# Chunk attention into a Swish layer: head order of the q and k loads, and the order of VectorE's work between TensorE's products

## The chip, the cores and the metric

The kernel runs on one core of a Trainium2 chip. The metric is the time of one execution in microseconds (us), as the device measures it; the span of a profile, from the first to the last instruction, is about 2 us shorter. TensorE multiplies matrices, VectorE (DVE in the profile), ScalarE (ACT) and GpSimd (POOL) work elementwise, and SyncE (SP) issues transfers. GpSimd issues transfers too. A run more than 1.5% above the fastest of its kernel is called slow and is left out of the ratios.

## The reference

```python
# q, k, v: [8 batches, 8 heads, 576, 64] float32, attention within chunks of 64 rows
scores = q_c @ k_c.T / 8
attn = softmax(scores)
x = (attn @ v_c)  -> [4608 tokens, 512]      # heads side by side
h = x @ w_in                                 # [512, 2048]
g = h / (1 + exp(-beta * h))                 # beta: [2048]
out = g @ w_out                              # [2048, 512], float32
```

## The kernel before

The tokens go through in nine blocks (`j`) of 512. A block has attention (scores, exp, a product with v, a division), 16 first-layer tiles (`emit_m`: four products of 128x512, then tanh on ScalarE and the gate on VectorE) and a second layer. Block 0 has a plain second layer; the others use a Strassen scheme: 7 groups of 16 products instead of 8, for which VectorE forms sums `s1` to `s4` of the gated tiles and GpSimd forms sums `tw` of the weights once. The loop puts the attention of block j+1 and the Strassen products of block j-1 into block j, at m = 4. A batch has 576 rows, a block 512.

```python
    def load_qk(b):
        ...
        for z in range(2):
            for src, dst in ((q, q_t), (k, k_t)):
                nc.gpsimd.dma_start(
                    out=dst[b][:, z].rearrange("p r d -> p (r d)"),
                    in_=src[b].rearrange("(a z) (t r) d -> z a t (r d)", z=2, r=RUN)[z],
                )
    ...
    def emit_sums(j, a, n):          # n = 4: four additions of 128x1024 in a row
        ...
        tt(out=s1[:, lo], in0=g[:, lo, dn], in1=g[:, hi, dn], op=ALU.add)
        tt(out=s2[:, lo], in0=s1[:, lo], in1=g[:, lo, up], op=ALU.subtract)
        tt(out=s3[:, lo], in0=g[:, lo, up], in1=g[:, lo, dn], op=ALU.subtract)
        tt(out=s4[:, lo], in0=g[:, hi, up], in1=s2[:, lo], op=ALU.subtract)
    ...
        def st6():                   # end of a block's Strassen products
            prod("A", s1, t1, False, True)
            o = ...                  # ScalarE: o = 0.5 * A
            put(1, 1, o)
            nc.gpsimd.tensor_tensor(out=w_, in0=sb["w1"], in1=o, op=ALU.add)
            put(0, 1, comb("C", w_)) # VectorE: waits for GpSimd
    ...
        for j in range(1, NB):
            at = attn(j + 1) if j + 1 < NB else []
            for m in range(KFF):
                if m == 4 and j >= 2:
                    for n, st in enumerate(steps_L2(j - 1)):
                        st()
                        if at and n < 6:
                            at.pop(0)()
                    if j + 2 < B:
                        for h2 in range(2):
                            emit_T(j + 2, h2)   # four q/k transposes on VectorE
                        ...                     # loads of batch j + 3
                if j == 1 and m >= 4 and at and m % 2 == 0:
                    at.pop(0)()
                emit_m(j, m)
                if m in (11, 15):
                    emit_sums(j, m - 11, 4)
```

The softmax here doesn't subtract the row's maximum and nothing guards it: scores larger than these inputs give would overflow.

## Time and profile before

| | before |
|---|---|
| time, median of the first 3 runs | 375.06 us |
| span of the profile | 373.1 us |
| TensorE / VectorE busy | 290.0 / 220.1 us |
| full-width first-layer products begin (block 0) | 29.3 us |
| first Strassen product | 110.4 us |
| from one block's first Strassen product to the next | 38.1 to 39.5 us in blocks 2 to 5, then 32.7 us, the last 24.6 us |

From the page of the kernel before: busy time of each engine with its share of the span, and the clock granted to TensorE in 40 slices, in tenths.

```profile
PE 290.0 (78%) x3296; PEld 173.5 (47%) x3296; DVE 220.1 (59%) x354; ACT 140.0 (38%) x216; POOL 83.8 (22%) x82
PEclk9999999569769989996999899989999999999999
```

No engine is full, and the clock falls again and again. What TensorE waited for, from the waits of the kernel before (engine and line, what released it: us in total, times, the longest):

```profile
PE hps L194 <- DVE gt L205: 23.8, 10, 3.9
PE sc L137 <- DVE kT L118: 19.0, 3, 14.3
PE oA L257 <- DVE gt L205: 10.4, 8, 1.4
```

The first-layer products (`hps`) and the first Strassen product (`oA`) wait for gates (`gt`), because a gate frees the PSUM bank that the next tile needs. The gates are late since VectorE does other things first. The timeline of the kernel before at one block's end shows them (start, us, engine, line, what, and in brackets the idle time before it and what ended it):

```profile
204.34 1.27 POOL L314 TENSOR_TENSOR w<-w,o 128x512 f32<-128x512 f32 x1 [3.19 <-issue]
205.64 0.69 DVE L275 SCALAR_TENSOR_TENSOR osb<-oC,w 128x512 f32<-128x512 f32 x1 [2.98 <-POOL w L314]
206.25 1.25 DVE L118 STREAM_TRANSPOSE qT<-qu 128x576 f32<-128x576 f32 x1
...
209.50 1.24 DVE L118 STREAM_TRANSPOSE kT<-ku 128x576 f32<-128x576 f32 x1
210.58 2.46 DVE L205 SCALAR_TENSOR_TENSOR gt<-sg,hps 128x512 f16<-128x512 f32 x4
211.31 8.75 PE L194 MATMUL hps<-xt,w_in 128*128 128x512 f16 x32 [3.90 <-DVE gt L205]
```

VectorE stands 2.98 us until GpSimd has its sum, combines, makes four transposes (4.3 us), and only then comes to the four gates that have been ready. TensorE is idle for 3.90 us. After that the clock is low, by the busy time in stretches (columns: stretch and its length, busy us of PE, PEld, DVE, ACT and POOL with instruction counts, granted clock, DMA share, GB/s):

```profile
211.30:214.70 3.40, 3.39 (x9) 1.27 (x9) 2.43 (x4) 1.38 (x2) 0.00 (x0) 0.53 0.97 158
```

The start, from the timeline of the kernel before: the first q is in VectorE's hands at 10.98 us.

```profile
10.98 1.26 DVE L118 STREAM_TRANSPOSE qT<-qu 128x576 f32<-128x576 f32 x1 [9.43 <-DMA qu<-in_q_dram]
29.33 16.26 PE L194 MATMUL hps<-xt,w_in 128*128 128x512 f16 x64 [0.52 <-DVE xt L181]
```

### The profile page before, as it was taken

What the parts mean: (1) busy time and instruction counts of PE and PEld (TensorE: products, weight loads), DVE (VectorE), ACT (ScalarE), POOL (GpSimd) and SP (SyncE); (2) the same over time, 40 slices, a digit from 0 to 9 for tenths busy, and PEclk for the clock granted to TensorE, in tenths of its full rate; (3) what the DMA queues carried; (4) which work ended last, traced back from release to release, by engine and by line L of the source; (5) the groups of instructions that cost most, each with busy time, mean ns of one, the idle gap of its engine ahead of it and who ended that gap; (6) DMA issues with size and microseconds to landing.
All of it is one profiled execution on the core that took longest, in us unless ns stands there. A gap on an engine that the chain in (4) does not pass through costs nothing.

```text
span 373.1 us, 7694 instructions
## 1 busy us (share of the span) xinstructions
PE 290.0 (78%) x3296; PEld 173.5 (47%) x3296; DVE 220.1 (59%) x354; ACT 140.0 (38%) x216; POOL 83.8 (22%) x82
## 2 busy tenths in 40 slices
PE   0149995479589867995889588958899699889893
PEld 0133442334138523862367136723674386367382
DVE  0544705387892579347852886378636934961951
ACT  1114701227323345332633263236427533633620
POOL 7324398513000520043002500110011002002002
PEclk9999999569769989996999899989999999999999
DMA  5999998699903599239912790320032023002002
GB/s 61 179 207 199 191 155 149 96 98 130 113 7 60 109 134 62 60 89 148 69 44 74 133 115 26 80 68 2 2 100 71 2 60 108 6 18 70 29 28 86
DMA packets 81827, 32.02 MB, mean 86 GB/s; under 512 B 65921, under 2 KB 76161, under 8 KB 81793
## 3 DMA queue, kind: packets, MB, share of 16 engines
q0 software_dynamic: 57216, 18.40, 48.7%
q1 hardware_dynamic: 24576, 13.12, 13.6%
q8 instruction: 26, 0.43, 0.5%
q14 instruction: 9, 0.07, 0.1%
HBM read 36.71 MB, written 9.44 MB: 124 GB/s over the span
## 4 chain that ended last, share of the span: by engine, by line
PE 48%; DVE 32%; issue 8%; ACT 4%; DMA 4%; POOL 3%; POOLq 0%; DVEq 0%
PE hps L194 17%; PE oA L257 13%; DVE gt L205 8%; PE oD L257 4%; PE oB L257 4%; DVE qT L118 4%; DMA vb<-in_v_dram 4%; DVE kT L118 3%; PE ops L323 3%; PE sc L137 3%; DVE s L219 3%; DVE x L167 3%; DVE s L220 3%; DVE s L222 2%; DVE s L221 2%
## 5 line engine op out<-in xcount | busy, mean ns | idle before, releaser
L194 PE MATMUL hps<-xt,w_in 128*128 128x512 f16 x576 | 144.6, 410 | 29.1 <-DVE gt L205 23.8
L202 ACT ACTIVATE sg<-hps,beta 128x512 f32<-128x512 f32 x144 | 99.0, 688 | 97.0 <-PE hps L194 55.9
L194 PEld LDWEIGHTS <-w_in 128*128 128x128 f16 x576 | 59.2, 104 | 108.8 <-issue 54.5
L205 DVE SCALAR_TENSOR_TENSOR gt<-sg,hps 128x512 f16<-128x512 f32 x144 | 93.0, 681 | 22.2 <-ACT sg L202 22.0
L302 POOL TENSOR_TENSOR w<-u,u 128x512 f32<-128x512 f32 x8 | 10.1, 1268 | 222.7 <-ACT u L268 222.7
L257 PEld LDWEIGHTS <-s 128*128 128x128 f16 x512 | 48.1, 98 | 6.3
L257 PE MATMUL oA<-tw,s 128*128 128x256 f16 x384 | 46.0, 273 | 0.0
L257 PEld LDWEIGHTS <-gt 128*128 128x128 f16 x384 | 36.5, 98 | 18.0 <-issue 12.6
L146 ACT ACTIVATE et<-sc 128x512 f16<-128x512 f32 x36 | 19.5, 594 | 44.9 <-PE sc L137 44.4
L137 PE MATMUL sc<-qT,kT 32*64 32x64 f16 x1152 | 14.6, 201 | 20.6 <-DVE kT L118 19.0
L268 ACT ACTIVATE u<-oA 128x512 f32<-128x512 f32 x24 | 14.3, 597 | 42.4 <-PE oA L257 42.4
L167 DVE TENSOR_TENSOR x<-x,rd 128x512 f16<-128x512 f32 x36 | 24.9, 691 | 1.2
L275 DVE SCALAR_TENSOR_TENSOR osb<-oD,u 128x512 f32<-128x512 f32 x8 | 5.5, 692 | 33.8 <-ACT u L268 33.8
L118 DVE STREAM_TRANSPOSE qT<-qu 128x576 f32<-128x576 f32 x16 | 19.9, 1241 | 9.4 <-DMA qu<-in_q_dram 9.4
L137 PEld LDWEIGHTS <-kT 32*64 32x64 f16 x1152 | 12.1, 114 | 25.1 <-DVE kT L118 19.3
L257 PE MATMUL oA<-w_out,gt 128*128 128x256 f16 x128 | 15.3, 272 | 10.4 <-DVE gt L205 10.4
L275 DVE SCALAR_TENSOR_TENSOR osb<-oC,w 128x512 f32<-128x512 f32 x8 | 5.5, 692 | 26.3 <-POOL w L314 26.3
L118 DVE STREAM_TRANSPOSE kT<-ku 128x576 f32<-128x576 f32 x16 | 19.8, 1236 | 0.8 <-DMA ku<-in_k_dram 0.8
L91 POOL DMA_DIRECT2D vb<-in_v_dram x16 | 18.7, 1173 | 5.6 <-DMA w_out<-in_moe_w_out_dram 5.4
L159 PE MATMUL x<-vb,et 64*64 64x65 f16 x576 | 13.3, 208 | 7.8 <-DVE x L167 3.3
L165 DVE RECIPROCAL rd<-x 128x8 f32<-128x8 f32 x36 | 7.3, 204 | 16.0 <-PE x L159 16.0
L159 PEld LDWEIGHTS <-et 64*64 64x64 f16 x576 | 8.6, 114 | 17.0 <-DVE x L167 6.7
(38 smaller groups left out, 192.4 us busy)
## 6 DMA issues: line engine op xcount, KB each, us to landing
out_dram<-osb SPq DMA_DIRECT2D x28, 256.0 KB, 2.2
qu<-in_q_dram POOLq DMA_DIRECT2D x16, 288.0 KB, 11.5
ku<-in_k_dram POOLq DMA_DIRECT2D x16, 288.0 KB, 11.7
vb<-in_v_dram POOLq DMA_DIRECT2D x16, 288.0 KB, 13.2
w_in<-in_moe_w_in_dram POOLq DMA_DIRECT2D x4, 512.0 KB, 15.7
w_out<-in_moe_w_out_dram POOLq DMA_DIRECT2D x4, 512.0 KB, 16.7
out_dram<-o SPq DMA_DIRECT2D x8, 256.0 KB, 4.1
xt<-x SPq DMA_TRANSPOSE x28, 2.3
```

The lines of the kernel that those rows point to most:

```text
L91: nc.gpsimd.dma_start(out=t[64 * hp:64 * hp + 64, :, :, 0:D].rearrange("p s c d -> p (s c) d"), in_=v[b, 4 * hp:4 * hp + 4].rearrange("s ( ...
L118: nc.vector.transpose(out=dst[b][:, h2].rearrange("p t r e -> p (t r e)").bitcast(FP32).rearrange("p (t r) -> p r t", r=RUN), in_=src[b][: ...
L137: nc.tensor.matmul(out=sc[a % 2][o0:o0 + 64, z, c, :], lhsT=kk[:, cb * CH:(cb + 1) * CH, e], rhs=qq[:, cb * CH:(cb + 1) * CH, e], start=(e ...
L146: nc.scalar.activation(out=et, in_=sc[s], func=ACTF.Exp, scale=scale)
L159: nc.tensor.matmul(out=x[o0:o0 + 64, hp, s, 0:D + 1], lhsT=et_t[g, a2][p0:p0 + 64, z, 2 * (i % 2) + cp, :], rhs=vbuf[b % NV][p0:p0 + 64, s ...
L167: nc.vector.tensor_tensor(out=x16, in0=x[:, :, :, 0:D], in1=rd.to_broadcast([128, 2, 4, D]), op=ALU.mult,)
L194: nc.tensor.matmul(out=hps, lhsT=w[:, kk, m // 2, m % 2, :], rhs=xt_t[j][:, kk, :], start=(kk == 0), stop=(kk == KDM - 1),)
L202: nc.scalar.activation(out=sg, in_=hps, func=ACTF.Tanh, scale=beta2[:, m % 2, m // 2:m // 2 + 1])
L205: nc.vector.scalar_tensor_tensor(out=gt_t[j][:, m, :], in0=sg, scalar=1.0, in1=hps, op0=ALU.add, op1=ALU.mult)
L219: tt(out=s1[:, lo], in0=g[:, lo, dn], in1=g[:, hi, dn], op=ALU.add)
L257: nc.tensor.matmul(out=bank[name][:, i, :], lhsT=a[:, kk, i * 128:(i + 1) * 128], rhs=b[:, kk, :], start=(first and i == 0 and kk == 0), s ...
L268: nc.scalar.activation(out=sb[name], in_=bank[src], func=ACTF.Copy, scale=0.5)
```

## The change

Four intents. Head order "(z a)" makes the source of a q or k load one 128-long dimension, which is meant to spread it over all 16 DMA engines. VectorE's sums are halved and given out one per gate; transposes and combinations stand each beside a group of Strassen products, and the C combination no longer waits for the last GpSimd sum. Batch 1's attention moves into block 0's plain second layer. All of w_in and w_out is loaded ahead of batch 1. The core of the diff (the head order also permutes w_in's rows and the indices of v; not shown either are the copies after TensorE's transposes, moved from VectorE to ScalarE, and two buffer counts):

```diff
-    def load_qk(b):
+    def load_qk(b, split=False):
...
-        for z in range(2):
+        for zs in ((slice(0, 1), slice(1, 2)) if split else (slice(0, 2),)):
             for src, dst in ((q, q_t), (k, k_t)):
                 nc.gpsimd.dma_start(
-                    out=dst[b][:, z].rearrange("p r d -> p (r d)"),
-                    in_=src[b].rearrange("(a z) (t r) d -> z a t (r d)", z=2, r=RUN)[z],
+                    out=dst[b][:, zs].rearrange("p z r d -> p z (r d)"),
+                    in_=src[b].rearrange("(z a) (t r) d -> (a t) z (r d)", z=2, r=RUN)[:, zs],
                 )
...
+        def cC():
+            comb("C", sb["w1"], keep="t")      # needs nothing of the last product
...
+            # mm6: out = t + o on GpSimd, on VectorE in the last block
...
+        emit_sc(0)
+        emit_sc(1, spare=True)                  # both score groups first, in spare PSUM
...
+        for m in range(2):
+            emit_h(0, m, 0, HT)                 # half-width products ahead of the last pv
+        emit_pv(3, True)
...
+        hooks = {                               # inside block 0's plain second layer
+            8: lambda: [T1[0](), T1[1]()], 9: lambda: [T1[2](), T1[3]()],
+            10: lambda: emit_sc(2), 12: lambda: emit_pv(4, True), 13: lambda: emit_pv(5, True),
+            14: lambda: emit_sc(3), 15: lambda: emit_pv(6, True),
+        }
...
+                    mm[0]()
+                    for p in range(4):
+                        emit_sum(j - 1, 3, p)
+                    if at:
+                        at[0]()
+                    if tr:
+                        tr.pop(0)()             # one transpose
+                    mm[1]()
+                    cB()
...
+                    mm[5]()
+                    if at:
+                        at[5]()
+                    cC()
+                    if tr:
+                        tr.pop(0)()
+                    mm[6]()
...
                 emit_m(j, m)
-                if m in (11, 15):
-                    emit_sums(j, m - 11, 4)
+                if m in (9, 11, 13, 15):
+                    fill += sums(j, (1, 2), ((m - 9) // 2,))
+                dve()                           # one 128x512 addition per gate
```

## The prediction

> **What bounds the kernel now.** The 373.1 us span falls into stages (chain of waits, timeline).
> - Start: the first q load is issued at 1.27 us and transposed only at 10.98; full-width first-layer products begin at 29.3. They end at about 45.4.
> - Block 0's plain second layer, then batch 1's attention exposed from 60.4 to 78.2 (17.8 us); TensorE's clock drops to 0.50 from 66 to beyond 80 us (busy time by stretch).
> - Block 1, 78.2 to the first Strassen product at 110.4: VectorE is busy 27.9 of 32 us.
> - Strassen products then start at 110.4, 148.5, 188.0, 226.5, 264.6, 297.3, 330.0, 354.6: about 38.5 us a block with q/k transposes, 32.7 without.
>
> A block needs of TensorE about 16 x 0.865 us (first layer) + 7 x 1.75 (products) + about 3 (attention) = 29 us. VectorE is busy 24.8 us of 38. Neither is full: they wait in turn. Four transposes (4 x 1.08) followed by late gates stop first-layer products for 3.9 us; a group of four sums stops them 1.4 us, twice a block; the GpSimd subtraction, with the combination behind it, holds a PSUM bank. So order on VectorE is the bound.
>
> **What the change does.**
> 1. With heads ordered (z a), partition is one 128-long dimension. The Trainium skill ("DMA: Bandwidth & Descriptors", "Why a DMA increments its semaphore by 16 and not by 1") says the slowest dimension sets the engine count, so 4 before and 16 after. The trace agrees so far: 63 GB/s at 4 to 6 us, 200 later. Estimate: all q/k of batch 0 landed by about 10.5 us, v by 14. Both score groups run first; attention's 2.0 us period per pv remains; w_in and w_out land before use. First-layer products end near 36 to 37 us: 9 saved.
> 2. Batch 1's attention sits inside the plain layer. TensorE stays warm but waits about 1.05 us per transpose by TensorE (as at 20.99 to 22.04). From first layer's end to block 1 falls from about 33 to 25 us: 8 saved.
> 3. Block 1 stays VectorE-bound: 8 transposes 8.6, 20 gates 12.4, sums 3, attention 3.4: about 27 us, less overlap. Saved 6 to 8, partly the cold clock.
> 4. Steady blocks: sums halved (0.61 us back to back for 1024; estimate 0.33 for 512), one per gate; transposes each beside a product of 1.75 us. VectorE's 12.4 us within the products' 15 us fits. Block: 29.2 us. Saved about 9.3 x 4 + 3.5 x 2 = 44.
> 5. Last block: 1.5 from better-placed sums, 1.3 from the final addition on VectorE instead of GpSimd (1.27 us).
>
> All of this is on the chain. Sum: first Strassen product near 86 us, + 6 x 29.2 + 23 + 17.2 = 301, plus 2 us between span and time = 303; I add 2 for waits not seen: **305 us, 297 to 319**. Faster by over 2%: 0.98; within: 0.01; slower: 0.01.
>
> **What would show it.** q transposed near 6 us; first-layer products ending near 37; no long hps wait on VectorE gates in steady state; product starts 29 to 30 us apart; mean clock near 1.0; VectorE busy total nearly the same (about 220 us) in a shorter span.
>
> **What would make it wrong.** pv products wait in TensorE's order on the single x bank, so a late VectorE would stop the whole pipeline: 31 us blocks add 11. Batch 1's or 3's q/k could land after their transposes. Starting attention may remain bound by v or exp. Too many sums per gate (0.95 against 0.865 us) could lag more than four PSUM banks absorb.

## The result, and the profile after

The changed kernel takes 317.41 us (median of 4 runs, 316.52 to 318.08) against 375.55 us before in the same rounds. The ratio is 0.8448, 95% interval 0.8417 to 0.8479. A ratio here is the mean time of one kernel's fast runs over that of the other's of the same rounds, so it is not quite the ratio of the quoted medians. Profiles compared below are of one execution: that of the changed kernel of its slowest (318.08 us), those of x1_win and u1_trans of their fastest, that of x2_t2 of its slowest.

The lines of the changed kernel that answer to those of before: busy times, clock, and the four largest of TensorE's waits.

```profile
PE 277.7 (88%) x3304; PEld 171.4 (54%) x3304; DVE 223.3 (71%) x410; ACT 144.4 (46%) x224; POOL 81.0 (26%) x83
PEclk9999999898995999999999999999999999999999
```

```profile
PE sc L147 <- DVE kT L121: 11.5, 2, 8.9
PE xps L188 <- DVE x L177: 8.9, 8, 1.5
PE hps L208 <- DVE gt L222: 4.3, 1, 4.3
PE hps L208 <- DMA w_in<-in_moe_w_in_dram: 3.5, 1, 3.5
```

VectorE does no less work. By the names of the profile the gates stop the first-layer products once, and a new wait for w_in stands where none was. In the chain of waits of the changed kernel the steady blocks are TensorE alone (start, us, what):

```profile
175.46 13.81 PE hps L208 x64
189.27 1.87 PE oA L281 x16
191.14 0.64 PE sc L147 x64
191.78 1.85 PE oB L281 x16
...
202.68 1.85 PE oA L281 x16
204.54 13.81 PE hps L208 x64
```

The period is 29.08 us (204.54 - 175.46), and all six steady distances lie within 0.01 us of it. Where the 56.8 us of span went, by the timelines of both:

| stretch | before | after | saved | predicted |
|---|---|---|---|---|
| to the end of block 0's first layer | 45.6 | 44.4 | 1.2 | 9 |
| from there to block 1's first product | 32.6 | 25.9 | 6.7 | 8 |
| block 1's first product to the first Strassen product | 32.2 | 31.7 | 0.5 | 6 to 8 |
| six steady distances | 219.6 | 174.5 | 45.1 | 44 |
| the last Strassen distance and the last block | 43.1 | 39.8 | 3.3 | about 3 |

The steady part came as predicted. The start and block 1 did not. In the start q came early, but something else was late (timeline of the changed kernel):

```profile
5.46 1.26 DVE L121 STREAM_TRANSPOSE qT<-qu 128x576 f32<-128x576 f32 x1 [4.06 <-DMA qu<-in_q_dram]
21.13 0.42 PE L208 MATMUL hps<-xt,w_in 128*128 128x256 f16 x1
25.07 1.65 PE L208 MATMUL hps<-xt,w_in 128*128 128x256 f16 x7 [3.51 <-DMA w_in<-in_moe_w_in_dram]
26.65 0.43 PE L169 MATMUL x<-vb,et 64*64 64x65 f16 x16
29.41 15.00 PE L208 MATMUL hps<-xt,w_in 128*128 128x256 f16 x64 [0.67 <-ACT xt L191]
```

One product of the first tile ran at 21.13 us, the second waited 3.51 us for a load of w_in. The two need columns of the same load. The chain of waits names the load that was issued at 11.09 us, which is the fourth of four:

```profile
11.09 13.84 DMA w_in<-in_moe_w_in_dram
```

The kernel's instruction list agrees: the first product of that tile waits for the semaphore of the first load alone, the second for those of the three others. In block 1 the timeline of the changed kernel shows the other wait:

```profile
92.34 0.69 DVE L177 TENSOR_TENSOR x<-x,rd 128x512 f16<-128x512 f32 x1
92.95 1.25 DVE L121 STREAM_TRANSPOSE kT<-ku 128x576 f32<-128x576 f32 x1
95.66 6.50 PE L208 MATMUL hps<-xt,w_in 128*128 128x512 f16 x16 [4.33 <-DVE gt L222]
```

The last x tile of block 2's attention leaves VectorE at 93.03 us, a DMA transpose takes it, and 2.63 us later block 2's first product starts. The profile names a gate, which ended at nearly the same moment; x4_t3 below, where the gates end earlier, has the same 2.63 us from tile to product, and there the profile names the DMA transpose. All the other variants of the changed kernel have it too (2.62 to 2.63 us). TensorE had been idle for 4.33 us, and the 16 products took 6.50 us instead of 3.5: the clock was 0.54 from 95.7 to 102.0 us, by the busy time in stretches:

```profile
95.70:102.00 6.30, 6.30 (x16) 2.18 (x17) 2.41 (x5) 2.06 (x3) 0.00 (x0) 0.54 0.00 0
```

The Trainium skill has a rule for this, in "TensorE: Matmul & The Clock Gate", section "What's actually happening": the clock falls to half after at least one idle window of about 3.4 us and returns after about one busy window. Two places agree: 0.53 after 3.90 us of idleness before, 0.54 after 4.33 us here. Others show it fall with less. In x1_win (below) it is 0.50 from 83.0 to 93.2 us, after a wait of 2.02 us, and the eight products behind that wait take 2.79 us, where the changed kernel takes 1.90 for eight behind the same wait. From the timeline of x1_win:

```profile
81.91 0.32 PE L169 MATMUL x<-vb,et 64*64 64x65 f16 x16 [2.02 <-DVE x L177]
82.16 2.79 PE L208 MATMUL hps<-xt,w_in 128*128 128x512 f16 x8
```

In the changed kernel's own plain layer it is 0.50 from 60.6 to 64.0 us, and no wait in the six us before was longer than 1.13 us. So no length of idleness alone decides it here; the measurement stands against the rule's limit. The traces do agree that the length of the slow time varies from run to run, as that section's note says: after the same idleness of 4.3 us the same 16 products took 6.50 us here, 5.12 in x2_t2 and 4.99 in x3_both.

For the same reason the length of block 1 in one profile says little. From its first product to the first Strassen product it is 31.7 us here and in u5_plain, 30.6 in u6_order, 30.2 in u7_comb_trans, 29.5 in x1_win and 28.5 in u1_trans, and none of these edits changes the order of work in block 1. The last x tile moves with the clock too: it leaves VectorE 21.0 us after the block's start where the clock is full until then or nearly so (x1_win, u1_trans), and 22.7 us where it is 0.50 for 3.4 us at or near the start (the changed kernel from 70.8 to 74.2, u7_comb_trans), later by half of the slow time.

### The profile page after: what moved, and what is told of

Read it like the earlier page. It is cut to its first block, busy times and chain, and to the rows that moved or that the text cites. A ratio compares the mean times of both kernels' runs of the same rounds, so it can differ in the third digit from the quotient of the medians.

```text
span 316.3 us, 7779 instructions
## 1 busy us (share of the span) xinstructions
PE 277.7 (88%) x3304; PEld 171.4 (54%) x3304; DVE 223.3 (71%) x410; ACT 144.4 (46%) x224; POOL 81.0 (26%) x83
## 4 chain that ended last, share of the span: by engine, by line
PE 82%; DVE 7%; DMA 7%; ACT 1%; issue 1%; POOL 0%; ACTq 0%; POOLq 0%
PE hps L208 39%; PE oA L281 19%; PE oB L281 5%; PE oC L281 5%; PE oD L281 5%; PE ops L358 4%; DMA w_in<-in_moe_w_in_dram 4%; PE sc L147 3%; DMA ku<-in_k_dram 2%; PE x L169 2%; DVE gt L222 2%; DVE x L177 2%; PE xps L188 1%; DVE kT L121 1%; DVE qT L121 1%
## 5 line engine op out<-in xcount | busy, mean ns | idle before, releaser
L208 PE MATMUL hps<-xt,w_in 128*128 128x512 f16 (+1 forms) x584 | 134.7, 392 | 9.2 <-DVE gt L222 4.3
L222 DVE SCALAR_TENSOR_TENSOR gt<-sg,hps 128x512 f16<-128x512 f32 x144 | 97.3, 683 | 28.3 <-ACT sg L219 28.2
L281 PEld LDWEIGHTS <-gt 128*128 128x128 f16 x384 | 36.5, 98 | 7.2 <-issue 1.5
L156 ACT ACTIVATE et<-sc 128x512 f16<-128x512 f32 x34 | 18.4, 594 | 35.9 <-PE sc L147 35.4
L93 POOL DMA_DIRECT2D vb<-in_v_dram x32 | 27.4, 872 | 11.2 <-DMA w_in<-in_moe_w_in_dram 3.6
L147 PE MATMUL sc<-qT,kT 32*64 32x64 f16 x1088 | 13.0, 198 | 11.5 <-DVE kT L121 11.5
L333 ACT ACTIVATE o<-oA 128x512 f32<-128x512 f32 x8 | 4.8, 597 | 27.8 <-PE oA L281 27.8
L358 PE MATMUL ops<-w_out,gt 128*128 128x512 f16 x64 | 16.2, 397 | 0.7 <-DVE gt L222 0.7
L169 PE MATMUL x<-vb,et 64*64 64x65 f16 x576 | 12.5, 203 | 3.5 <-DVE x L177 2.3
L281 PE MATMUL oB<-w_out,gt 128*128 128x256 f16 x128 | 15.4, 273 | 0.0
L281 PE MATMUL oC<-w_out,s 128*128 128x256 f16 x128 | 15.3, 273 | 0.0
```

What stands on the lines that cost most here:

```text
L93: nc.gpsimd.dma_start(out=t[64 * hp:64 * hp + 64, 2 * z:2 * z + 2, :, 0:D].rearrange("p s c d -> p (s c) d"), in_=v[b, h0:h0 + 2].rearrang ...
L147: nc.tensor.matmul(out=sc[a % 2][o0:o0 + 64, z, c, :], lhsT=kk[:, cb * CH:(cb + 1) * CH, e], rhs=qq[:, cb * CH:(cb + 1) * CH, e], start=(e ...
L156: nc.scalar.activation(out=et, in_=sc[s], func=ACTF.Exp, scale=scale)
L169: nc.tensor.matmul(out=x[o0:o0 + 64, hp, s, 0:D + 1], lhsT=et_t[g, a2][p0:p0 + 64, z, 2 * (i % 2) + cp, :], rhs=vbuf[b % NV][p0:p0 + 64, s ...
L208: nc.tensor.matmul(out=hps_t[j, m][:, c0:c1], lhsT=w_r[:, 2 * z + e, m // 2, m % 2, :], rhs=xt_t[j][:, n, c0:c1], start=(n == 0), stop=(n ...
L222: nc.vector.scalar_tensor_tensor(out=gt_t[j][:, m, :], in0=sg, scalar=1.0, in1=hps, op0=ALU.add, op1=ALU.mult)
```

## The experiments

Names that begin with x try to mend the changed kernel, with u undo one part of the change, and b1_heads does one part alone on the kernel before. All were correct. "First" is the start of the first Strassen product in the profile, "distance" is from one block's to the next. "First" varies by some 4 us with identical code before it (102.0, 100.2, 98.2 and 98.3 in the changed kernel, u6_order, u1_trans and u7_comb_trans); the ratios, of four runs each, are the safer measure.

| run | median us | ratio to before | first | distance |
|---|---|---|---|---|
| changed kernel | 317.41 | 0.8448 | 102.0 | 29.1 |
| x1_win | 311.94 | 0.8305 | 94.2 | 29.1 |
| x2_t2 | 314.73 | 0.8377 | 101.2 | 29.1 |
| x3_both | 313.42 | 0.8299 | 94.1 | 29.1 |
| x4_t3 | 314.35 | 0.8347 | 98.6 | 29.1 |
| u1_trans | 323.19 | 0.8575 | 98.2 | 30.5 (four), 29.1 |
| u2_sums | 338.04 | 0.897 | 102.3 | 32.1 |
| u4_heads | 332.62, fast runs 329.4 | 0.8758 | 105.4 | 29.1, 33.7, 36.5, 31.7, 29.1 (slow run) |
| u5_plain | 325.07 | 0.8649 | 110.4 | 29.1 |
| u6_order | 317.22 | 0.8425 | 100.2 | 29.1 |
| u7_comb_trans | 344.18 | 0.9166 | 98.3 | 35.1 to 36.4 (four), 29.5 |
| b1_heads | 372.03 | 0.989 | 107.2 | as before |
| best | 302.41 | 0.8052 | 86.1 | 29.1 |

### x1_win: w_in in four tiles

```diff
-    w_in16 = big.tile([128, KDM, DFF], FP16)
+    w_in16 = [big.tile([128, KDM, DFF // 4], FP16, name=f"w_in{g}") for g in range(4)]
...
-                lhsT=w_r[:, 2 * z + e, m // 2, m % 2, :],
+                lhsT=w_r[m // 4][:, 2 * z + e, (m // 2) % 2, m % 2, :],
```

> Changed kernel with w_in held in four separate tiles, one per load, instead of one tile. Theory 1 (false wait): the second first-layer product of block 0 waited at 21.6 to 25.1 us for the FOURTH w_in load, because the waits are worked out on address ranges of one tile and the row of k=2 falls inside the range of every load; with separate tiles it waits for the first load only, which is long in: the 3.5 us wait goes, time 317.4 to about 314 (313 to 315). Rival (bandwidth): the four loads share the 16 engines and finish together near 25 us; then the wait stays at over 2.5 us and the time is within 1 us of the changed kernel.

311.94 us, 5.4 us less by the ratios ((0.8448 - 0.8305) times 376). That is more than the 313 to 315 expected. The wait is gone; the timeline of x1_win:

```profile
21.13 1.92 PE L208 MATMUL hps<-xt,w_in 128*128 128x256 f16 x8
25.73 14.41 PE L208 MATMUL hps<-xt,w_in 128*128 128x256 f16 x64 [0.67 <-ACT xt L191]
```

So the first load was in by 21 us, and the wait for the other three was false: in one tile the row of k = 2 lies between the first and the last byte of every load. It was passed on in full, since the last pv product, which had its data, stood behind it in TensorE's order: the 64 products that follow start 3.7 us sooner (25.73 against 29.41). (The Trainium skill, same page, "Step-by-step: what each phase is for", says that products stay in program order and only weight loads are pulled ahead; the pv at 26.65 us above agrees.) The times of this kernel lie in two pairs, 310.4 and 313.5 to 313.9, so its gain is known only to about 2 us; the mended wait is certain, and what goes beyond it (block 1 in 29.5 us instead of 31.7) is no more than identical code varies by.

### x2_t2: less VectorE work at the head of block 1

```diff
-            10: lambda: emit_sc(2), 12: ...
+            10: lambda: [emit_sc(2), T2[0](), T2[1]()], 11: lambda: [T2[2](), T2[3]()], 12: ...
...
-            if j == 1:
-                for f in T_items(2):
-                    f()
```

> Changed kernel with the four transposes of batch 2 moved from the head of block 1 into the plain layer of block 0, where VectorE is idle over 10 us. Theory: in block 1 VectorE's backlog makes the last x tile late (93.0 us), a 2.4 us DMA transpose follows, TensorE idles 4.3 us and then runs 6.2 us at clock 0.55; taking 4.4 us off VectorE removes 4 to 8 us: 309.5 to 313.5. Rival: block 1 is bound by TensorE or by batch 3's loads; then under 1.5 us changes.

314.73 us, about 2.7 us less: neither theory's number. The wait that was to go stayed (timeline of x2_t2), and from block 1's first product at 69.81 to the first Strassen product at 101.15 it is 31.3 us, as against 31.7 in the changed kernel.

```profile
92.87 0.69 DVE L177 TENSOR_TENSOR x<-x,rd 128x512 f16<-128x512 f32 x1
93.48 1.25 DVE L121 STREAM_TRANSPOSE kT<-ku 128x576 f32<-128x576 f32 x1
96.19 5.12 PE L208 MATMUL hps<-xt,w_in 128*128 128x512 f16 x16 [4.32 <-DVE gt L222]
```

This speaks against the theory that the amount of VectorE work bounds block 1: 4.4 us of it were taken away at the head, and the last x tile was not earlier: it leaves VectorE 23.75 us after the block's start, which is the 21.0 us of a full clock and half of the 5.6 us for which the clock is 0.50 at the start of this block. VectorE was idle early in the block and crowded late, where three transposes still stood before that tile. Where the 2.7 us come from was not settled: the profile is of the slowest run (317.25 us), the other three took 314.5 to 314.9 with a higher mean clock (0.987 to 0.993 against 0.982), and none of them was profiled.

### x3_both

> Both edits. If the two waits are independent, the gains add: 306 to 310. If they overlap (an earlier block 0 only meets the loads or the GpSimd products of weights sooner), about the better one of the two alone.

313.42 us, ratio 0.8299 against 0.8305 for x1_win alone: the gains do not add, and on top of x1_win x2's edit is worth nothing. With it and without it the last x tile leaves VectorE 21.0 us after the block's start (profiles of x3_both and x1_win), which again speaks against the amount of work. The first of the two expectations, 306 to 310, was a miss; the second, about the better edit alone, held. One of the four runs was slow and is left out of the ratio.

### x4_t3: same work, other order

```diff
                 if j == 1 and m >= 4 and m % 2 == 0 and at:
                     at.pop(0)()
-                    if m >= 8 and tr:
-                        tr.pop(0)()
```

> Changed kernel with batch 3's four transposes moved from between block 1's gates to after its last gate; batch 2's stay at its head, so VectorE has the same work. After x2_t2 showed that 4.4 us less work at the head moved nothing, the theory is order: the last x tile of block 1 stands behind three transposes in VectorE's queue, then a DMA transpose of about 2.6 us, and TensorE waits 4.3 us. Now the tile is ready about 3 us earlier and the transposes run while TensorE waits: the first Strassen product comes 3 to 5 us after block 1's start sooner, time 312 to 315. Rival: amount of VectorE work between block start and Strassen product is what counts; then unchanged, 316 to 318.

314.35 us, 3.8 us less by the ratios, as expected; its four runs (311.6 to 314.6) lie under all eight of the changed kernel and u6_order (316.3 to 318.1). From block 1's first product (70.26) to the first Strassen product it is 28.3 us instead of 31.7, but u1_trans has 28.5 with block 1 unchanged, so this length alone shows nothing. The tile's place does: it leaves VectorE 20.6 us after the block's start, against 22.7 in the changed kernel's profile, which has the same slow clock there (0.50 from 70.8 to 74.1 us in x4_t3, to 74.2 in the changed kernel). The timeline of x4_t3 shows the tile earlier and the transposes in TensorE's wait:

```profile
90.13 0.69 DVE L177 TENSOR_TENSOR x<-x,rd 128x512 f16<-128x512 f32 x1
92.72 1.25 DVE L121 STREAM_TRANSPOSE qT<-qu 128x576 f32<-128x576 f32 x1
93.45 5.30 PE L208 MATMUL hps<-xt,w_in 128*128 128x512 f16 x16 [3.25 <-DMA xt<-x]
```

The tile is ready at 90.82 us (90.13 + 0.69), and 2.63 us later the product starts. Now the profile itself names the DMA transpose as what ended the wait. TensorE still idles 3.25 us, and its products are still slow (5.30 us), because attention's last step stands at m = 14 of 16.

### u1_trans: transposes in a row

```diff
-                    if tr:
-                        tr.pop(0)()        # at four places
...
                     mm[6]()
+                    while tr:
+                        tr.pop(0)()
```

> Changed kernel with the four transposes of a batch issued in a row after the last Strassen product, as before, all else kept. Theory: each of the four blocks that has them (2 to 5) waits about 3.5 us on late gates again (4.3 us of VectorE work, less the free banks), product starts 32 to 33 us apart there, 29.1 elsewhere: 327 to 335. Rival: the gain came from the sums alone and four PSUM banks absorb the transposes: under 321.

323.19 us: 4.8 us more by the ratios, between the two expectations. The four blocks take 30.5 us instead of 29.1. TensorE waits 1.26 us a block for a gate, not 3.5, as the timeline of u1_trans shows for each of the four:

```profile
118.25 10.52 PE L208 MATMUL hps<-xt,w_in 128*128 128x512 f16 x48 [1.26 <-DVE gt L222]
```

The clock does not fall in these blocks (of this profile, the fastest of four runs). With the combination out of the way the transposes begin at the products' end, and the free banks cover most of their 4.3 us.

### u2_sums: sums in two groups of four

```diff
-                if m in (9, 11, 13, 15):
-                    fill += sums(j, (1, 2), ((m - 9) // 2,))
-                dve()
+                if m in (11, 15):
+                    for w in (1, 2, 3, 4):
+                        emit_sum(j, w, (m - 11) // 4)
...
 # slices of 4 tiles instead of 2 (128x1024 each); the calls for sums 3 and 4 between the products go
```

> Changed kernel with the sums in two groups of four 128x1024 additions a block, as before, all else kept. Theory: each group stops first-layer products about 1.4 us, twice a block in eight blocks: about +20, 330 to 341. Rival: only together with the grouped transposes did they matter, and the banks absorb a group of 2.4 us: under 323.

338.04 us, 20 us more by the ratios; every steady block takes 32.1 us, 3.0 more, and the last distance is 24.1 instead of 22.6. The waits of u2_sums show the 1.4 us of before again, twice a block:

```profile
PE oA L281 <- DVE gt L222: 10.0, 7, 1.4
PE hps L208 <- DVE gt L222: 8.2, 6, 1.4
```

### u7_comb_trans: transposes in a row, behind a combination that waits for GpSimd

```diff
 # u1_trans, and in mm6:
-            nc.gpsimd.tensor_tensor(out=o2, in0=sb["t"], in1=o, op=ALU.add)
-            store(j, 0, 1, o2)
+            nc.gpsimd.tensor_tensor(out=w_, in0=sb["w1"], in1=o, op=ALU.add)
+            store(j, 0, 1, comb("C", w_))
...
         def cC():
-            comb("C", sb["w1"], keep="t")
+            pass
```

> u1_trans, and the C combination again behind the GpSimd addition, as before. u1_trans alone cost only 1.4 us a block. Theory: before, VectorE stood at this combination until GpSimd was done (about 3 us) and only then began the transposes, and the gates came after both: the two waits are in series, so blocks 2 to 5 become 33 to 36 us instead of 30.5: 331 to 345. The blocks without transposes only pay under 1 us. Rival: the combination is no cause; then 321 to 326.

344.18 us, in the expected range. The blocks with transposes take 35.1 to 36.4 us, those without 29.5. The combination alone is thus worth 0.4 us a block and the transposes alone 1.4, but both together 6.1 to 7.3. The timeline and a stretch of u7_comb_trans repeat the kernel before:

```profile
151.90 0.69 DVE L300 SCALAR_TENSOR_TENSOR osb<-oC,w 128x512 f32<-128x512 f32 x1 [2.98 <-POOL w L336]
...
157.57 4.65 PE L208 MATMUL hps<-xt,w_in 128*128 128x512 f16 x13 [3.90 <-DVE gt L222]
```

```profile
157.50:161.00 3.50, 3.43 (x9) 1.30 (x9) 2.49 (x5) 1.37 (x2) 0.00 (x0) 0.54 1.65 186
```

The same 2.98 us, the same 3.90 us, the same low clock. One after another the two delays outlast the free banks, and the idleness is now long enough to drop the clock, which neither alone is. With 3.0 us for the sums this gives 29.1 + 3.0 + 6.1 to 7.3 = 38.2 to 39.4 us for a block with transposes and 29.1 + 3.0 + 0.4 = 32.5 for one without. The kernel before has 38.1 to 39.5 and 32.7. So the steady gain is accounted for, if the sums add to the other two; no run undoes all three at once.

### u4_heads and b1_heads: the head order

u4_heads puts the old `load_qk`, `load_v` and indices back into the changed kernel; b1_heads puts the new ones into the kernel before.

```diff
 # u4_heads, against the changed kernel; b1_heads makes the opposite edit to the kernel before
-                    in_=src[b].rearrange("(z a) (t r) d -> (a t) z (r d)", z=2, r=RUN)[:, zs],
+                    in_=src[b].rearrange("(a z) (t r) d -> z a t (r d)", z=2, r=RUN)[z],
```

> Changed kernel with the old head order and so the old four-dimensional q/k loads, all else kept. Theory: it is worth only the start, where q is transposed at 11 instead of 5.5 us and scores end about 4 us later; steady blocks hold data one block ahead and stay at 29.1 us: 320 to 323. Rival: narrow loads also come late for block 1 or for the steady blocks: over 326.

> The kernel BEFORE with only the new head order (q and k loads on one 128-long dimension, v and w_in rows to match). u4_heads cost 12 us, of which about 5 at the start and the rest in blocks 3 to 5, whose transposes, now spread among the products, waited for q. Theory: that second part exists only because the change starts the transposes of a batch about 14 us after its loads are issued; in the kernel before they start after all products, so the loads are long in. Then the head order alone moves only the start: 3 to 6 us faster, 370 to 373, and the product starts of blocks 3 to 6 stay 38 to 39.5 us apart. Rival: narrow loads hold up the steady blocks of the kernel before as well: under 366, and those distances fall by 2 us or more.

u4_heads costs 12 us (fast runs 329.35 and 329.52; ratio 0.8758 against 0.8448), where 3 to 6 were expected. b1_heads gains 4.1 us, as expected, and leaves the steady distances of the kernel before as they were (38.2, 39.6, 38.5, 38.1). So the head order is worth three times as much after the rest of the change as before it. The only profile of u4_heads is of a slow run; in it the first layer's end is 5 us later than in the changed kernel, and in three blocks the first transpose waits for q (3.4, 5.2 and 3.0 us), as in this line of its timeline:

```profile
176.76 1.25 DVE L118 STREAM_TRANSPOSE qT<-qu 128x576 f32<-128x576 f32 x1 [5.17 <-DMA qu<-in_q_dram]
```

VectorE is ready for q there at 171.6 us, 13 us after the loads' issue began at 158.7. The narrow q loads of 288 KB take 15.0 us to land (median of that run), the wide ones of 576 KB 7.4 us (median in the changed kernel). In the kernel before the transposes come after all Strassen products, when the loads are long in. That explains the difference, but the wait itself was seen in a slow run alone, so its size in the fast ones is argued, not shown.

### u5_plain and u6_order

u5_plain runs the hooks after the plain layer; u6_order puts batch 1's q and k between the first and the other w_out loads, as before.

```diff
 # u5_plain
         for kk, f in enumerate(mm):
-            if kk in hooks:
-                hooks[kk]()
             f()
         fin()
+        for kk in sorted(hooks):
+            hooks[kk]()
```

> Changed kernel with batch 1's transposes and attention after the plain layer of block 0, as before, all else kept. Theory: the exposed attention returns, TensorE idles and its clock falls to 0.5: +6 to +11, 323 to 329. Rival: the plain layer was stretched by what was put into it (23 us instead of 15), so little is lost: under 320.

> Changed kernel with the load order of before: batch 1's q and k between the first and the other three pieces of w_out. Theory: w_out has over 8 us of slack before the plain layer at 46 us, and batch 1's transposes too, so nothing changes: 317.4 within 1 us. Rival: the order is part of the gain; then later w_out pieces stop the plain layer, 319 or more.

u5_plain: 325.07 us, 7.6 us more by the ratios, as expected and as step 2 predicted. u6_order: 317.22 us, no change. The part of the change that puts all weights ahead of batch 1 is worth nothing here.

### best: what the experiments point to

```diff
 # x1_win, and:
+            6: lambda: emit_sc(2), 8: lambda: emit_pv(4, "later"),
+            9: lambda: [turns[4](), emit_pv(5, "later"), T2[0]()],
+            10: lambda: [turns[5](), T2[1]()], 11: lambda: emit_sc(3),
+            13: lambda: emit_pv(6, "later"),
+            14: lambda: [turns[6](), emit_pv(7, "later")],
+            15: lambda: [turns[7](), T2[2](), T2[3]()],
...
-        emit_tw()
         load_qk(3)
+        emit_tw()
...
-                for f in T_items(2):
-                    f()
+                while tr:                       # batch 3
+                    tr.pop(0)()
...
-                if j == 1 and m >= 4 and m % 2 == 0 and at:
+                if j == 1 and m % 2 == 1 and at:
                     at.pop(0)()
-                    if m >= 8 and tr:
-                        tr.pop(0)()
```

Here `"later"` leaves a tile's TensorE transposes to `turns[i]`, one step on.

> Changed kernel with separate w_in tiles; batch 1's attention started earlier in the plain layer with each TensorE transpose one step after its pv product; batch 2's transposes in the plain layer; batch 3's q/k loaded before the GpSimd products of weights and transposed at the head of block 1; block 1's attention at m = 1, 3, ..., 11. Theory: w_in wait gone (4 to 5), plain layer 4 to 6 shorter, block 1 without the last-tile wait and the cold clock (6 to 8): 296 to 304. Rival: the gains overlap because w_out or batch 1's loads bind next: 306 to 311.

302.41 us (302.10 to 303.71), ratio 0.8052: 15 us under the changed kernel, and inside the expected range. The first Strassen product starts at 86.1 us instead of 102.0, the mean clock is 0.990 instead of 0.978, and what TensorE waits for after the start has shrunk; from the waits of best:

```profile
PE xps L190 <- DVE x L179: 4.3, 5, 1.0
PE hps L215 <- DVE gt L229: 2.8, 2, 2.0
```

## Why the prediction was right or wrong

The time, 317.4 us, lies inside the range of 297 to 319 us, and the direction was sure. It lies 12 us above the point and 1.6 us under the upper end, so the range held narrowly: two of the five steps were wrong.

1. **Start (step 1), wrong in size: 9 us predicted, 1.2 measured.** The loads came sooner, as step 1 had it. The Trainium skill ("DMA: Bandwidth & Descriptors", "Why a DMA increments its semaphore by 16 and not by 1") has the engine count follow from the slowest dimension, and the first q load landed after 4.2 us instead of 9.4 (shortest q load of each profile), with 180 GB/s coming in from 4 to 6 us instead of 63; the number of engines itself is not in these traces. What failed is "w_in and w_out land before use". The first piece did land before use, but the products waited for all four, and x1_win shows that this wait was not needed. It accounts for about 4 of the 8 us missed (the first layer ends at 40.1 us in x1_win, at 44.4 here). The rest was not taken apart; two things seen are that the first pv was held up for v until 15.35 us, not 14, and that the 15.00 us of the products at the end are more than a whole first layer takes in steady state (13.81).
2. **Plain layer (step 2), right in size: 8 predicted, 6.7 measured;** u5_plain gives 7.6 by undoing it. "TensorE stays warm" was not so throughout: the clock was 0.50 from 60.6 to 64.0 us.
3. **Block 1 (step 3), wrong: 6 to 8 predicted, 0.5 measured.** The failed words are "Block 1 stays VectorE-bound ... about 27 us". I added up VectorE's work and took the sum for the time. What sets the block's length is one tile's place in VectorE's queue, the DMA transpose behind it, and the last 16 products, slowed by a clock that falls in the meantime: 22.7 + 2.6 + 6.3 = 31.7 us. x2_t2 and x3_both took 4.4 us of work away and the tile was no earlier; x4_t3 took none away, and with the same clock the tile was 2.1 us earlier and the time 1.2% shorter; best, with attention begun at m = 1, has the block in 26.3 us. "Partly the cold clock" failed as well: the clock was 0.50 again for 3.4 us at the block's start and while the last products ran. In this profile that costs about 1.7 us (half of 3.4) and 2.9 us (6.3 instead of the 3.45 of best).
4. **Steady blocks (step 4), right: 29.2 us a block predicted, 29.08 measured; 44 us saved predicted, 45.1 measured.** The parts are not what a sum of single effects would say: sums 3.0 a block (u2_sums), combination 0.4, transposes 1.4, the last two together 6.1 to 7.3 (u1_trans, u7_comb_trans). I had read the transposes' 3.9 us wait as theirs alone.
5. **Last block (step 5), right: about 3 us.** Two runs undo its terms apart: u2_sums lengthens the last distance by 1.5 us (1.5 predicted), and u7_comb_trans, which also puts the last block's final addition back on GpSimd and the combination behind it, lengthens the time from the last Strassen block's start to the end by 1.35 us (18.61 against 17.26; 1.3 predicted).

The signs that I had named: q transposed at 5.46 us (right), first layer ending near 37 (wrong, 44.4), no long gate waits in steady state (right), 29 to 30 us between product starts (right), clock near 1.0 (0.978), VectorE about 220 us busy (223.3). Of the dangers, late q and k did not happen, except with the old loads in u4_heads, and there for later batches. The false wait and the clock loss in block 1 were not on my list; together they used up most of the range.

## What to carry to other kernels

The place of an instruction in an engine's queue mattered more here than the engine's total: find the one result that the next engine waits for, and see what stands before it in the queue. Two delays that free buffers hide singly can cost several times their sum when they come one after another, above all if TensorE's clock then falls as well. When one tile is filled by several loads and rows of it interleave, give each load its own tile, and check which load a product really waited for. And before a stretch of one profile is compared with that of another, see how far it varies where the code is the same: here block 1 did by 3 us.

## What the Trainium skill lacked or had wrong

- No page has it that a product can wait for loads that it does not read, because several strided loads fill one tile: 3.5 us of wait and 5.4 us of time (known to about 2), gone with a tile for each load (x1_win).
- "DMA: Bandwidth & Descriptors" says to put a dimension that is a multiple of 16 outermost, but not what a narrow load costs in time to landing: 9.4 us for the shortest q load of the old layout, 4.2 for that of the new one (both 288 KB); and that four narrow loads in flight together lose less: the last of the first four was transposed at 15.19 us before and at 10.83 after.
- "TensorE: Matmul & The Clock Gate", "What's actually happening", ties the fall of the clock to an idle window of about 3.4 us. Here it also fell after a single wait of 2.02 us (x1_win), and in the changed kernel's plain layer where no wait was over 1.13 us; in x1_win it then stayed at 0.50 for 10.2 us. The waits of 1.3 to 1.4 us in the steady blocks of u1_trans and u2_sums did not make it fall.
- The same section puts the warm-up's cost at under 1% of a typical kernel, which is for a clock that rises once. In blocks 2 to 5 of u7_comb_trans it fell in each block: in the one shown, the 13 products after the wait took 4.65 us, where 13 at the steady rate (13.81 us for 64) take 2.8, which is 1.8 us of a 36 us block, 5%.
